# Attention and a routed expert layer on one core: two-sided buckets, spare matmuls, V loads behind q, new planner costs, and two expert tiles moved into the attention

## The chip, the cores and the metric

The kernel runs on one core of a Trainium2 chip. TensorE (PE) multiplies, VectorE (DVE) and ScalarE (ACT) work on vectors, GpSimd (POOL) and SyncE (SP) here mostly issue DMAs; POOL has its own DMA queue (the software one), SP another. The metric is device time in microseconds of one execution, lower is better.

## The reference

q, k, v are (8 batches, 8 heads, 576 tokens, 64) in float32. The attention is causal by blocks of 64. Its output, one row of 512 values for each of 4608 tokens, goes through a layer of 8 experts of which each token takes two:

```
scores = (q @ k^T) / 8, where block(i) >= block(j), else -1e9
x = softmax(scores) @ v            # (4608, 512)
noisy = x @ w_gate + log1p(exp(x @ w_noise)) * noise      # (4608, 8)
two largest per token, their softmax = weights
out[t] = sum over both experts e: weight * (relu(x[t] @ w1[e]) @ w2[e])   # 512 -> 1024 -> 512
```

## The kernel before, in words

A class `Plan` (L19 to L153) is a list scheduler inside the kernel: every step is added with an engine, a cost in microseconds, a key (smaller goes first), what it comes after, and the places it takes or gives back in pools. `order` plays this through and emits all instructions in one fixed order for each engine. On the chip each engine follows its order and waits where something is late; the costs matter only through the order that they make.

**Attention.** Eight batches b0 to b7, two halves (b0 to b3, b4 to b7), pairs pb = b // 2. For a batch, POOL issues the loads of q and k (`load_qk` L328, L330, the last 64 tokens in `load_rest` L335) and SP those of V (`load_v` L342, L345); PE turns q and k (`turn` L385, `turn_rest` L404), ACT or DVE copy the turned tiles (L395, L397); PE makes scores (L435, L453), ACT their exponentials (L444, L459), DVE clears the masked blocks (L465), POOL or DVE cast V (L353), PE multiplies with V (`av_mm` L480, L490), DVE divides (L500). The buffers `raw` for q and k number four, so two batches of them. V of b0 is loaded at once.

**Routing.** Of each batch x is turned (L512), copied (L521), and multiplied with the gate (L530). With each second batch the pair's 1152 tokens are routed on DVE (top2 L554 to L562, rows L583 to L592, shares L607 to L613) with `places` on PE (L569), which counts the tokens ahead of each one in its expert. Then POOL issues 18 scatters of 128 rows (`scatter` L627), 72 in all, into one bucket per expert and half in device memory (`xd`, 640 rows = five tiles, filled from row 0). The rows from 512 on are cleared first (`clear_x` L640).

**Experts.** 16 steps (half, e), in the order (0,0), (0,1), (0,2), (0,3), (1,0) to (1,3), (0,4), (1,4) and so on. A step loads its bucket (`load_x`, SP, L652), after all scatters of its half; PE turns it (`row_turn` L660), ACT or DVE copy (L670, L672); layer 1 is eight groups of 4 x 2 matmuls of 320 columns (L718), each with a relu (L727); layer 2 is, for each of five tiles, eight matmuls of 512 columns (L734). For every tile the result is scaled and stored (`y_early` L742 on ACT, two of them on DVE, `y_store` L749) if the expert is not the last, and, if it is not the first, the result that the token's other expert stored is gathered (`gather` L756, POOL), added (`y_late` L767, DVE) and written to the output rows (`y_out` L774, POOL). Rows for which a tile is the wrong side are dropped by an index out of bounds. So 70 tiles are stored, 70 gathered, 70 written out. A flag (L789 on) sends the program into a second, slow branch (L816) if a bucket overflowed.

What sets the order around the change: the keys of `load_qk`, `load_v` and `scatter`, the rule that a step is emitted when its inputs are ready by the planned costs, and in-order queues. In the places where PE works for experts before the attention is over there is nothing: no expert step starts before its half is scattered.

## Time and profile before

| what | value |
|---|---|
| three timed runs | 466.64, 472.96, 477.19 us (median 472.96) |
| profiled execution | 466.68 us, span 465.0 us, mean granted PE clock 0.971 |
| PE busy | 421.0 us, 91% of the span |
| ACT, POOL, DVE busy | 274.8, 272.7, 196.0 us |
| DMA moved | 96.24 MB, mean 207 GB/s |

The page gives each engine's busy time over one span, the span in 40 slices, the DMA queues, the chain that ended last, and the costliest groups of instructions by line. The windows cut the span at times that can be chosen. The attention ends at about 157 us; the expert steps without it run from there to the last matmul at 458 us.

### The profile page before, as it was taken

The page shows a single profiled execution, that of the slowest core. Times are in us where ns is not written, and L with a number is a line of the kernel's source. Part 1 is how long each engine was busy: PE and PEld are TensorE (multiplying, and loading weights), DVE is VectorE, ACT ScalarE, POOL GpSimd, SP SyncE. Part 2 cuts the span into 40 slices and gives each one's busy share as a digit, 9 for nine tenths or more (in the row PEclk, how much of TensorE's full clock was granted, in tenths as well). Part 3 has the DMA queues.
Part 4 walks back from the last instruction along what each step waited for, and adds up shares of the span by engine and source line. Part 5 has one row for each costly group of instructions (what it writes and reads, how often), then busy time and mean ns, then how long its engine had stood idle before and what let it go on. Part 6 is the DMA issues. An engine that isn't in the chain of part 4 may idle for free.

```text
span 465.0 us, 11045 instructions
## 1 busy us (share of the span) xinstructions
PE 421.0 (91%) x4409; PEld 271.9 (58%) x4431; DVE 196.0 (42%) x516; ACT 274.8 (59%) x364; POOL 272.7 (59%) x311
## 2 busy tenths in 40 slices
...
GB/s 164 185 168 189 241 239 223 204 200 222 192 249 236 226 271 247 296 146 229 208 200 203 211 152 188 181 218 219 291 225 271 303 169 207 229 147 228 135 65 102
DMA packets 108858, 96.24 MB, mean 207 GB/s; under 512 B 62944, under 2 KB 83424, under 8 KB 108800
## 3 DMA queue, kind: packets, MB, share of 16 engines
...
q14 instruction: 22, 0.18, 0.1%
...
## 4 chain that ended last, share of the span: by engine, by line
PE 65%; DMA 12%; DVE 10%; ACT 5%; issue 4%; POOL 2%; SPq 2%; POOLq 0%; DVEq 0%; ACTq 0%
PE yp L734 27%; PE hp L718 26%; DMA row<-xd 7%; ACT esc L444 4%; PE tr L660 3%; PE av L480 3%; DVE xr L500 2%; DMA raw<-in_q_dram 2%; PE sc L435 2%; DMA nz_all<-in_moe_noise_dram 2%; DVE Tq L397 2%; DMA vst<-in_v_dram 1%; POOL out_dram L774 1%; PE tr L385 1%; PE av L490 1%
## 5 line engine op out<-in xcount | busy, mean ns | idle before, releaser
L718 PE MATMUL hp<-xg,w 128*128 128x320 bf16 x1024 | 147.4, 299 | 0.1
L734 PE MATMUL yp<-w,hsb 128*128 128x512 bf16 x618 | 140.3, 379 | 1.2
L727 ACT ACTIVATE hsb<-hp 128x640 bf16<-128x640 f32 x127 | 89.4, 704 | 59.3 <-PE hp L718 58.1
L718 PEld LDWEIGHTS <-w 128*128 128x128 bf16 x1024 | 98.8, 98 | 39.9 <-issue 0.3
L734 PEld LDWEIGHTS <-hsb 128*128 128x128 bf16 x640 | 62.2, 97 | 73.3 <-issue 3.5
L444 ACT ACTIVATE esc<-sc 128x1024 bf16<-128x1024 f32 x96 | 92.3, 1027 | 15.1 <-PE sc L435 6.0
L627 POOL DMA_INDIRECT xd<-xr,slots x72 | 71.4, 992 | 35.0 <-issue 18.6
L774 POOL DMA_INDIRECT out_dram<-yobuf,trow x42 | 41.2, 980 | 29.1 <-DVE yobuf L767 20.7
L742 ACT ACTIVATE ybuf<-yp,wrow 128x512 f32<-128x512 f32 x42 | 28.9, 687 | 43.2 <-PE yp L734 43.2
L672 DVE COPY xg<-tr 128x1024 bf16<-128x1024 bf16 (+1 forms) x28 | 16.2, 577 | 87.9 <-PE tr L660 87.9
L774 POOL DMA_INDIRECT out_dram<-xr,trow x28 | 28.3, 1011 | 41.4 <-DVE xr L767 29.0
L756 POOL DMA_INDIRECT gbuf<-yd,grow x34 | 35.0, 1029 | 25.6 <-DMA yd<-xr 13.8
L435 PE MATMUL sc<-Tq,Tk 64*128 64x512 bf16 (+4 forms) x320 | 39.7, 326 | 9.9 <-ACT esc L444 7.2
L756 POOL DMA_INDIRECT xr<-yd,grow x36 | 37.1, 1030 | 11.8 <-issue 10.6
L480 PE MATMUL av<-vt,esc 128*128 128x65 bf16 x640 | 33.0, 208 | 9.0 <-DVE xr L500 4.7
L480 PEld LDWEIGHTS <-esc 128*128 128x128 bf16 x640 | 26.5, 106 | 20.4 <-DVE xr L500 6.5
L500 DVE TENSOR_TENSOR xr<-av,rden 128x256 bf16<-128x256 f32 (+1 forms) x80 | 33.9, 424 | 3.9 <-DMA xd<-xr,slots 1.0
L742 ACT ACTIVATE xr<-yp,wrow 128x512 f32<-128x512 f32 x26 | 17.9, 688 | 27.8 <-PE yp L734 25.7
L385 PE MATMUL tr<-ident,raw 128*64 128x128 bf16 x512 | 22.5, 239 | 10.5 <-POOL tok_i L304 7.3
L767 DVE SCALAR_TENSOR_TENSOR yobuf<-yp,wrow,xr 128x512 f32<-128x512 f32 x22 | 16.5, 751 | 26.4 <-ACT xr L742 17.6
L385 PEld LDWEIGHTS <-raw 128*64 128x64 bf16 x512 | 17.7, 120 | 14.8 <-DMA raw<-in_q_dram 8.3
L767 DVE SCALAR_TENSOR_TENSOR yobuf<-yp,wrow,gbuf 128x512 f32<-128x512 f32 x20 | 15.0, 750 | 25.0 <-ACT xr L742 13.8
...
## 6 DMA issues: line engine op xcount, KB each, us to landing
...
```

Source lines behind the costliest of these rows:

```text
L385: nc.tensor.transpose(tp[64 * f:64 * f + 64, r * P:(r + 1) * P], raws[b, x][:, o:o + D], ident)
L435: nc.tensor.matmul(out=sc[:, f, off:off + z - a], lhsT=kT[sl, m * S + jt * P:m * S + (jt + 1) * P], rhs=qT[sl, m * S + a:m * S + z], start ...
L444: nc.scalar.activation(out=escs[b, st][:, mm, :, piece * 512:(piece + 1) * 512], in_=scs.pop((b, m, piece)), func=AF.Exp, scale=scale)
L480: nc.tensor.matmul(out=av[:, f, mm, :], lhsT=esc[:, mm, f, c:c + P], rhs=vb[:, jt, h, :], start=(jt == 0), stop=(jt == idx))
L500: nc.vector.tensor_tensor(out=xrs[b // 2][sl, t, 0:Dm].rearrange("p (f m d) -> p f m d", f=2, m=HP)[:, :, 2 * st:2 * st + 2], in0=av[sl, : ...
L627: ins = nc.gpsimd.indirect_dma_start(out=xd[half].bitcast(I32), out_offset=bass.IndirectOffsetOnAxis(ap=slots[:, pb * TG + t, i:i + 1], ax ...
L718: nc.tensor.matmul(out=hp[:, n, 0:NW], lhsT=wload[e, 1][:, db, fb * P:(fb + 1) * P], rhs=xgs[half, e][:, db, n * NW:(n + 1) * NW], start=( ...
L727: nc.scalar.activation(out=o, in_=i, func=AF.Relu)
L734: nc.tensor.matmul(out=yp, lhsT=hs[half, e][:, fb, c * P:(c + 1) * P], rhs=wload[e, 2][:, fb, :], start=(fb == 0), stop=(fb == FB - 1))
L742: nc.scalar.activation(out=t, in_=yps[half, e, c], func=AF.Copy, scale=w)
L756: ins = nc.gpsimd.indirect_dma_start(out=g, out_offset=None, in_=yd[half][0:e * CAP], in_offset=bass.IndirectOffsetOnAxis(ap=grow[half][:, ...
L774: ins = nc.gpsimd.indirect_dma_start(out=out, out_offset=bass.IndirectOffsetOnAxis(ap=trow[half][:, e, c:c + 1], axis=0), in_=yos.pop((hal ...
```

## The change

Each token now has a lower and a higher expert (`roles`). In the lower one's bucket it fills rows from the bottom, in the higher one's from the top (places with a sign, `sg`). So a tile of a bucket holds rows of one kind, and limits by expert (`TE`, `TL`) say which tiles are stored and which gathered: 23 of each half, 46 in all, where there were 70. The stored rows lie closer (`YB`). The gap in the middle of a bucket is cleared (160 rows, `GAP`), in b0 and b4. A bucket beyond these limits sends the program into the slow branch.

The planner gets a hop by engine, starting times, and lower PE costs. Where PE would stand idle by the plan, and before the first turn, it puts in a `spare` matmul of ones, 128x512, into the PSUM tile that the next step takes (52 in all, 14 of them ahead of the first turn; the last is in the middle of b5). V of b0 waits for q's second chunk (the other wait, `RV`, is set so that it never applies). Pair 0's scatters get a later key and pair 1's an earlier one, against the other work on POOL. `FIRST = ((0, 2),)`: after pair 0's scatters SP loads the first two tiles of expert 0, half 0 (`load_first`); they are turned, and go through layer 1 (32 matmuls of 256 columns) and layer 2, in b5 to b7; the step (0,0) then does three tiles.

```diff
-    HOP = 0.08
+    HOP = {None: 0.0, "PE": 0.2, "ACT": 0.16, "DVE": 0.13, "POOL": 0.12, "SP": 0.08}
...
+    BEGIN = {"SP": 0.8, "DVE": 1.0, "POOL": 1.3, "ACT": 2.1}
...
-    ZR = 512
+    CR = 160
+    TL = (0, 1, 2, 3, 3, 4, 5, 5)
+    TE = TL[::-1]
+    YB = [P * sum(TE[:e]) for e in range(E + 1)]
...
+    FIRST = tuple((e, n) for e, n in ((0, 2), (1, 0)) if n)
...
+            if (b, idx) == (0, 0):
+                tc.add_manual_dep(ins.ins, loads[0, "q", 1].name, SYNC_DEP, reason="the first q and k go first")
...
+    begun = {}
+
+    def av_tile(name):
+        return begun.pop("av", None) or av_ps.tile([P, 512], F32, tag="av", name=name)
+
+    def sc_tile(name):
+        return begun.pop("sc", None) or sc_ps.tile([P, 2, 512], F32, tag="sc", name=name)
+
+    def spare(x):
+        if x not in begun:
+            begun[x] = av_tile("sp") if x == "av" else sc_tile("sp")
+        o = begun[x] if x == "av" else begun[x][:, 0]
+        nc.tensor.matmul(out=o, lhsT=ones_mat, rhs=ones_mat.unsqueeze(1).to_broadcast([P, 4, P]), start=True, stop=True)
...
+    def roles(pb):
+        r = rs["p", pb]
+        cd = rt.tile([P, 2, TG, E], BF16, tag="cd", name="cd")
+        nc.vector.tensor_tensor(out=cd, in0=r["oh"], in1=code.to_broadcast([P, 2, TG, E]), op=ALU.mult)
+        cc = rt.tile([P, 2, TG], F32, tag="cc", name="cc")
+        nc.vector.reduce_sum(cc, cd, axis=AX.X)
+        sel = rt.tile([P, TG, 2, 1], F32, tag="sel", name="sel")
+        nc.vector.tensor_tensor(out=sel[:, :, 0, 0], in0=cc[:, 0], in1=cc[:, 1], op=ALU.min)
+        nc.vector.tensor_tensor(out=sel[:, :, 1, 0], in0=cc[:, 0], in1=cc[:, 1], op=ALU.max)
+        sg = rt.tile([P, TG, 2, E], BF16, tag="sg", name="sg")
+        nc.vector.tensor_tensor(out=sg, in0=sel.to_broadcast([P, TG, 2, E]), in1=code.to_broadcast([P, TG, 2, E]),
+                                op=ALU.is_equal)
+        nc.vector.tensor_scalar(sg[:, :, 1], sg[:, :, 1], -1.0, None, op0=ALU.mult)
+        r.update(sg=sg, cc=cc)
...
-        pp = av_ps.tile([P, TG, E], F32, tag="av", name="pp")
-        nc.tensor.matmul(out=pp, lhsT=prem, rhs=m, start=True, stop=False)
+        sg = r["sg"].rearrange("p t i e -> p t (i e)")
+        pp = av_tile("pp")[:, 0:2 * TG * E].rearrange("p (t e) -> p t e", t=TG)
+        nc.tensor.matmul(out=pp, lhsT=prem, rhs=sg, start=True, stop=False)
         for t in range(TG - 1):
             nc.tensor.matmul(out=pp[:, t + 1:TG, :], lhsT=ones_mat,
-                             rhs=m[:, t:t + 1, :].to_broadcast([P, TG - 1 - t, E]), start=False, stop=False)
...
+        pk = rt.tile([P, TG, 2, E], F32, tag="pk", name="pk")
+        nc.vector.tensor_tensor(out=pk, in0=r["sg"], in1=r["pp"].rearrange("p t (i e) -> p t i e", i=2), op=ALU.mult)
         sl2 = rt.tile([P, TG, 2], F32, tag="sl2", name="sl2")
-        nc.vector.reduce_sum(sl2.rearrange("p t i -> p i t"), pk, axis=AX.X)
-        rec = xrs[pb][:, :, Dm:DR].bitcast(I32)
-        nc.vector.tensor_copy(slots[:, g0:g0 + TG, :], sl2)
-        nc.vector.tensor_copy(rec[:, :, 0:2], sl2)
+        nc.vector.reduce_sum(sl2, pk, axis=AX.X)
+        nc.vector.scalar_tensor_tensor(out=slots[:, g0:g0 + TG, :], in0=sl2, scalar=-1.0, in1=sl2,
+                                       op0=ALU.mult, op1=ALU.max)
+        nc.vector.tensor_copy(xrs[pb][:, :, Dm:DR].bitcast(I32)[:, :, 0:2], slots[:, g0:g0 + TG, :])
...
+    GAP = [min(max(4 * (S // 4 * (E - 1 - e) // (E - 1)) - 48, 0), CAP - CR) for e in range(E)]
 
     def clear_x(half, e):
-        flat = xd[half].rearrange("(e r) c -> e r c", e=E)[:, ZR:CAP, :].rearrange("e (p a) c -> e p (a c)", a=4)
-        nc.sync.dma_start(out=flat[e], in_=zeros[e % 4])
+        r0 = e * CAP + GAP[e]
+        nc.sync.dma_start(out=xd[half][r0:r0 + CR, :].rearrange("(p a) c -> p (a c)", a=4), in_=zeros[e % 2])
...
+    def load_first():
+        t = row_pool.tile([P, CT * Dm], BF16, tag="row", name="row")[:, 0:len(early) * DR].rearrange("p (c d) -> p c d", d=DR)
+        rowss["first"], mine = t, []
+        for e, n in FIRST:
+            k = early.index((e, 0))
+            ins = nc.sync.dma_start(out=t.bitcast(I32)[:, k:k + n, :], in_=xd[0].bitcast(I32)[e * CAP:e * CAP + n * P, :]
+                                    .rearrange("(c p) d -> p c d", p=P))
+            mine.append(ins.ins)
+            for nm in scat_of[0]:
+                tc.add_manual_dep(ins.ins, nm, SYNC_DEP, reason="rows landed")
+        for i in mine:
+            tc.add_to_no_dep_group("scat0", i)
...
+    def load_x(half, e, c0):
         t = row_pool.tile([P, CT, Dm], BF16, tag="row", name="row")
-        landed(nc.sync.dma_start(out=t, in_=xd[half][e * CAP:(e + 1) * CAP, 0:Dm]
+        landed(nc.sync.dma_start(out=t[:, c0:CT, :], in_=xd[half][e * CAP + c0 * P:(e + 1) * CAP, 0:Dm]
...
+    def layer1(half, e, fb, c0, c1):
+        if fb == 0 and c0 == 0:
             hs[half, e] = h_pool.tile([P, FB, CAP], BF16, tag="hsb", name="hsb")
-        hp = sc_ps.tile([P, 2, 512], F32, tag="sc", name="hp")
+        hp = sc_tile("hp")
         for db in range(DB):
-            for n in range(2):
...
+                nc.tensor.matmul(out=hp[:, i, 0:n], lhsT=wload[e, 1][:, db, fb * P:(fb + 1) * P],
+                                 rhs=xgs[half, e][:, db, a:a + n],
                                  start=(db == 0), stop=(db == DB - 1))
...
     def y_store(half, e, c):
-        r0 = e * CAP + c * P
+        r0 = YB[e] + c * P
...
     def gather(half, e, c):
         g = spot("g")
         ins = nc.gpsimd.indirect_dma_start(
-            out=g, out_offset=None, in_=yd[half][0:e * CAP],
+            out=g, out_offset=None, in_=yd[half][0:YB[e]],
             in_offset=bass.IndirectOffsetOnAxis(ap=grow[half][:, e, c:c + 1], axis=0),
-            bounds_check=e * CAP - 1, oob_is_err=False)
+            bounds_check=YB[e] - 1, oob_is_err=False)
...
-                pe = add("PE", 0.58, lambda b=b, x=x, c=c: turn(b, x, c), after=[turned[x, c], o_new, o_ident],
+                key = u0 + 3 * c * (b == 0) - 5
+                pe = add("PE", 0.46, lambda b=b, x=x, c=c: turn(b, x, c), after=[turned[x, c], o_new, o_ident],
...
-                s = rest[b] = add("PE", 0.4, lambda b=b: scores_rest(b), key=key, take=["sc"], after=list(got.values()))
+                s = rest[b] = add("PE", 0.25, lambda b=b: scores_rest(b), key=key, take=["sc"], after=list(got.values()))
...
-                pe = add("PE", (0.22, 0.33, 0.45, 0.56, 0.68)[idx], lambda b=b, st=st, idx=idx: av_mm(b, st, idx),
-                         after=need_v + [mk], key=key + 3 + 0.1 * idx, take=["av"])
+                pe = add("PE", (0.12, 0.24, 0.35, 0.47, 0.6)[idx], lambda b=b, st=st, idx=idx: av_mm(b, st, idx),
+                         after=need_v + [mk], key=key + 2 + 0.1 * idx, take=["av"])
...
-            if b == (1, 2)[hf]:
-                cleared[hf] = [add("SP", 0.3, lambda hf=hf, e=e: clear_x(hf, e), key=u0 - 10 + e,
-                                   after=[units[b, (2, 0)], o_vec], xfer=(0.41, 165)) for e in range(E)]
+            if b == (0, 4)[hf]:
...
+            t2 = add("DVE", 1.3, lambda pb=pb: top2(pb), after=[noi[b - 1], noi[b], o_cast], key=kr - 20)
+            ro = add("DVE", 0.9, lambda pb=pb: roles(pb), after=[t2], key=kr - 20)
...
-            ss = [add("POOL", 1.28, lambda pb=pb, t=t, i=i: scatter(pb, t, i), after=[routed, *cleared[half]], key=kr + (0, 20, 10, 0)[pb],
+            ss = [add("POOL", 1.28, lambda pb=pb, t=t, i=i: scatter(pb, t, i), after=[routed, *cleared[half]], key=kr + (20, -30, 0, 0)[pb],
                       xfer=(0.36, 165))
...
-    weights(0, lambda: wE, [units[2, (m, 0)] for m in range(4)], unit(6, 0), calm=1)
-    weights(1, lambda: wE, [units[5, (m, 0)] for m in range(4)], unit(6, 0) + 1, calm=2)
+        ra = add("DVE", 0.9, lambda half=half: read_rec_a(half), key=unit(6, 0), after=[lr, done_b[half], o_cast])
+        rec_ops[half] = add("DVE", 1.2, lambda half=half: read_rec_b(half), key=unit(6, 0), after=[ra])
+    weights(0, lambda: wE, [units[3, (m, 0)] for m in range(4)], unit(6, 0), calm=4)
+    weights(1, lambda: wE, [units[6, (m, 0)] for m in range(4)], unit(6, 0) + 1, calm=4)
...
-    weights(3, lambda: wl["R"], [scat_ops[1][18 + n] for n in (0, 3, 6, 9)], unit(6, 0) + 3, [o_right], calm=4)
+    weights(3, lambda: wl["R"], [scat_ops[1][18 + n] for n in (4, 7, 10, 13)], unit(6, 0) + 3, [o_right], calm=4)
...
-        kb = 1000 + 20 * sn
-        lx = add("SP", 1.0, lambda half=half, e=e: load_x(half, e), key=unit(6, 6) + sn, take=["row"],
-                 after=scat_ops[half], behind=[last_x], xfer=(2.0, 45), late=1.0)
+        kb = 1000 + 20 * sn - (0 if sn == 0 else 900 if sn == 1 else 0)
+        cut = dict(FIRST).get(e, 0) if half == 0 else 0
+        if sn == 0 and cut:
+            first_x = add("SP", 1.0, load_first, key=unit(2, 6), after=scat_ops[0][0:2 * TG], take=["row"], xfer=(1.2, 60), late=1.0)
...
+            used = [first_w]
+        lx = add("SP", 1.0, lambda half=half, e=e, cut=cut: load_x(half, e, cut), key=unit(5, 6) + sn, take=["row"],
+                 after=scat_ops[half], behind=[last_x], xfer=(0.4 * (CT - cut), 45), late=1.0)
...
-        o_x = add(None, 0, key=kb, take=["xg"], after=[lx, last_xg])
+        o_x = add(None, 0, key=kb, take=["xg"], after=[first_x if cut else lx, last_xg])
...
-            pl.ops[r]["fn"] = lambda half=half, e=e, j=j, r=r: row_copy(half, e, j, pl.ops[r]["by"])
-            xcs.append(r)
...
+        for c0, c1 in ((0, cut), (cut, CT)) if cut else ((0, CT),):
...
+                n = min(2, c1 - j)
+                cs = list(range(j, j + n))
+                pe = add("PE", 0.225 * n, lambda half=half, e=e, cs=cs: row_turn(half, e, cs), key=kb - 15 + 0.05 * j,
+                         after=[first_x if c1 <= cut else lx, o_x], take=["tr"])
...
+            w = (c1 - c0) / CT
+            rl[c0] = []
+            for fb in range(FB):
+                pe = add("PE", 0.02 + 1.07 * w, lambda half=half, e=e, fb=fb, c0=c0, c1=c1: layer1(half, e, fb, c0, c1),
+                         key=kb + fb + 0.1 * c0, after=[*xcs, *wop[e][1], o_h], take=["sc"])
+                l1.append(pe)
...
-        if e:
-            for c in range(CT):
+        if TL[e]:
+            for c in range(CT - TL[e], CT):
                 gs[c] = add("POOL", 1.32, lambda half=half, e=e, c=c: gather(half, e, c), key=kb + c, take=["g"],
                             after=st_ops[half] + [rec_ops[half]], behind=[last_g], xfer=(0.5, 85), late=2.2)
...
         for c in range(CT):
             pe = add("PE", 1.75, lambda half=half, e=e, c=c: layer2(half, e, c), key=kb + 10 + c,
-                     after=rl + wop[e][2], behind=[last_2], take=["av"])
+                     after=rl[cut if c >= cut else 0] + wop[e][2], behind=[last_2] if c >= cut else [], take=["av"])
...
             fin = []
-            if e < E - 1:
-                ye = add(("ACT", "DVE") if sn < 4 else "ACT", (0.6, 0.75) if sn < 4 else 0.6, None, after=[pe, rec_ops[half]], key=500 + kb + c, take=["y"])
+            if c < TE[e]:
+                ye = add(("ACT", "DVE") if sn < 4 else "ACT", (0.6, 0.75) if sn < 4 else 0.6, None, after=[pe, first_w if c < cut else rec_ops[half]], key=500 + kb + c, take=["y"])
...
-            if e:
+            if c >= CT - TL[e]:
                 yl = add("DVE", 0.75, lambda half=half, e=e, c=c: y_late(half, e, c),
                          after=[pe, gs[c], rec_ops[half]], key=500 + kb + c, take=["yo"], give=["g"])
```

**PE, start of the program.** `raw` is q and k as loaded, `sp` the spare tile. Before:

```order
L1275 UNCONDITIONAL_BRANCH
L385 LDWEIGHTS raw
L385 MATMUL tr<-ident,raw 64x128
```

Now:

```order
L1406 UNCONDITIONAL_BRANCH
L419 LDWEIGHTS ones_mat
L419 MATMUL sp<-ones_mat 128x512
...
L426 LDWEIGHTS raw
L426 MATMUL tr<-ident,raw 64x128
```

Fourteen spare matmuls stand ahead of the first turn.

**POOL, the loads of q and k for b5 to b7 and the scatters.** `xd` is the bucket, `raw` and `rest` are q and k, `w` expert weights. Before, from pair 0's scatters on (the first loads are those of b5):

```order
L627 DMA xd<-xr,slots 5120x260 x18
L328 DMA raw<-in_q_dram 128x2x1024
L328 DMA raw<-in_k_dram 128x2x1024
L335 DMA rest<-in_q_dram 32x2x512
L335 DMA rest<-in_k_dram 32x2x512
...
L627 DMA xd<-xr,slots 5120x260 x3
...
L627 DMA xd<-xr,slots 5120x260 x9
L328 DMA raw<-in_q_dram 128x2x1024
L328 DMA raw<-in_k_dram 128x2x1024
L627 DMA xd<-xr,slots 5120x260 x6
```

Now:

```order
L681 DMA xd<-xr,slots 5120x260 x9
L350 DMA raw<-in_q_dram 128x2x1024
L350 DMA raw<-in_k_dram 128x2x1024
L681 DMA xd<-xr,slots 5120x260 x9
L360 DMA rest<-in_q_dram 32x2x512
...
L681 DMA xd<-xr,slots 5120x260 x18
L350 DMA raw<-in_q_dram 128x2x1024
L350 DMA raw<-in_k_dram 128x2x1024
```

The loads of b5 stand behind nine of pair 0's scatters instead of 18; those of b7 behind all 18 of pair 1's instead of twelve. Between the two pieces shown last stand the loads of b6 and four of weights.

**PE, the first tiles of expert 0 inside the attention** (now; before there is nothing of the kind). `sc` are scores, `esc` their exponentials, `xg` turned rows, `hp` the hidden layer:

```order
L476 MATMUL sc<-Tq,Tk 128x192
L737 LDWEIGHTS row
L737 MATMUL tr<-ident,row 128x128
...
L521 LDWEIGHTS esc
L521 MATMUL sp<-vt_140,esc 128x65
...
L800 LDWEIGHTS w_1556
L800 MATMUL hp<-xg,w_1556 128x256
```

Eight turns stand together in b5, 32 matmuls of layer 1 spread over the end of b6, 16 of layer 2 in two groups in b7.

## Rows read from the trace of the kernel before

**Rows 1.** Section 1 of the page: busy time, share of the span, instructions.

```profile
PE 421.0 (91%) x4409; PEld 271.9 (58%) x4431; DVE 196.0 (42%) x516; ACT 274.8 (59%) x364; POOL 272.7 (59%) x311
```

**Rows 2.** Windows: us, PE, PEld, DVE, ACT, POOL busy, PEclk, DMA, GB/s.

```profile
0.00:157.50 157.50, 122.48 (x2357) 88.85 (x2358) 112.72 (x345) 119.58 (x146) 88.78 (x124) 0.92 1.05 209
176.00:458.00 282.00, 280.73 (x1848) 170.55 (x1868) 73.56 (x132) 146.10 (x205) 168.84 (x172) 1.00 0.76 206
458.00:465.00 7.00, 0.31 (x2) 0.00 (x0) 0.75 (x1) 0.00 (x0) 1.59 (x2) 0.75 0.18 61
```

**Rows 3.** Lines by form, whole span: count | busy us, mean ns | idle before.

```profile
L587 DVE TENSOR_TENSOR pk<-oh,pos 128x144 f32<-128x144 bf16 x4 | 1.2, 307 | 0.1
L459 ACT ACTIVATE esc<-sc 128x256 bf16<-128x256 f32 x8 | 3.1, 385 | 0.0
L727 ACT ACTIVATE hsb<-hp 128x640 bf16<-128x640 f32 x127 | 89.4, 704 | 59.3 <-PE hp L718 58.1 <-PE fs L805 0.4
L742 ACT ACTIVATE ybuf<-yp,wrow 128x512 f32<-128x512 f32 x42 | 28.9, 687 | 43.2 <-PE yp L734 43.2
L756 POOL DMA_INDIRECT gbuf<-yd,grow x34 | 35.0, 1029 | 25.6 <-DMA yd<-xr 13.8 <-issue 11.7
```

**Rows 4.** The chain of waits: start, us, engine, tile, line, in the dense stage.

```profile
205.23 8.41 PE yp L734 x38
213.65 6.52 PE hp L718 x48
...
220.16 0.89 PE tr L660 x16
```

**Rows 5.** Timeline at the end, POOL: start, us, engine, operation.

```profile
459.38 0.97 POOL L774 DMA_INDIRECT out_dram<-yobuf,trow  x1 [0.76 <-DVE yobuf L767]
```

**Rows 6.** Timeline at the start, SP, POOL, PE, ACT.

```profile
0.82 3.15 SPq L342 DMA_DIRECT2D vst<-in_v_dram  x4
1.36 0.90 POOL L330 DMA_DIRECT2D raw<-in_q_dram  x1 [0.83 <-POOLq L1264]
7.26 1.06 PE L385 MATMUL tr<-ident,raw 128*64 128x128 bf16 x16 [7.26 <-POOL tok_i L304]
13.67 1.07 PE L385 MATMUL tr<-ident,raw 128*64 128x128 bf16 x16
13.74 1.94 ACT L444 ACTIVATE esc<-sc 128x1024 bf16<-128x1024 f32 x2
16.67 0.62 POOL L353 CAST vt<-vst 128x512 bf16<-128x512 f32 x1
21.07 0.84 PE L480 MATMUL av<-vt,esc 128*128 128x65 bf16 x12
```

**Rows 7.** Timeline, loads of q and k, scatters, ACT's waits, a turn.

```profile
90.53 0.78 POOL L328 DMA_DIRECT2D raw<-in_q_dram  x1
96.50 1.08 POOL L627 DMA_INDIRECT xd<-xr,slots  x1 [0.76 <-DVE ms L612]
100.62 1.02 ACT L395 ACTIVATE Tq<-tr 128x1024 bf16<-128x1024 bf16 x1 [2.46 <-PE tr L385]
106.27 4.69 ACT L444 ACTIVATE esc<-sc 128x1024 bf16<-128x1024 f32 x5 [1.35 <-PE sc L435]
107.40 1.07 POOL L627 DMA_INDIRECT xd<-xr,slots  x1 [0.30 <-issue]
118.86 0.78 POOL L328 DMA_DIRECT2D raw<-in_q_dram  x1
130.93 0.64 PE L385 MATMUL tr<-ident,raw 128*64 128x128 bf16 x16
```

**Rows 8.** Windows in which the granted clock was low, columns as in group 2.

```profile
92.50:103.50 11.00, 9.35 (x138) 7.03 (x135) 7.69 (x31) 7.26 (x9) 6.32 (x9) 0.53 1.14 199
123.50:127.50 4.00, 3.83 (x62) 3.08 (x59) 2.98 (x10) 2.35 (x3) 3.09 (x4) 0.57 1.15 207
137.00:144.50 7.50, 6.89 (x108) 4.90 (x109) 6.11 (x27) 4.70 (x6) 3.10 (x4) 0.54 1.15 226
```

326 lines of the change are left out of this document (190 added, 136 removed).

## The prediction, made blind

> **What bounds the kernel now.** I read the busy times first, then the windows by stage, then the chain of waits, then the timeline of the places that the change touches. PE is busy 421.0 us and no other engine over 275 [rows 1], but that is a mean over two different stages. In the stretch 176 to 458 us PE works 280.73 of 282 us at the full granted clock, while ACT has 146.1 and POOL 168.8 [rows 2]: the expert steps are bound by PE alone, and the chain runs through their matmuls there [rows 4]. In the attention, 0 to 157.5 us, nobody is full: PE 122.5, ACT 119.6, DVE 112.7, POOL 88.8, DMA share 1.05 and 209 GB/s, mean clock 0.92 [rows 2]. The reader should see from this that a piece of work taken from ACT, POOL or SP after 176 us is worth nothing, a matmul taken from there is worth its time, and what changes in the attention is worth what its own chain says.
>
> **The sum** is made against the profiled execution (466.68 us, span 465.0). The median of the three timed runs, 472.96, lies 6.3 above it; as the runs reach from 466.6 to 477.2 I add half of that, 3.1, to a profiled time.
>
> *Fewer stores, gathers and writes of y.* 24 tiles less of each: 24 evictions of 0.69 us on ACT, 24 gathers of 1.03 and about as long a write each on POOL [rows 3, 5], some 49 us of POOL. All of it lies under the 280.73 us of PE; POOL has 113 us free there [rows 2]. **0.** At the end the last matmul is over before the stretch 458 to 465, and what follows (an addition, writes from POOL, the last 0.97 long at 459.38, their landing) remains [rows 2, 5]: 0 as well. If the cover were gone, two writes in the tail would cost 2 us.
>
> *The first two tiles.* The dense stage loses 8 turns (16 take 0.89, so 0.45), two fifths of layer 1 of one step (eight groups of 8 matmuls: 48 matmuls take 6.52 us, so 64 take 8.7 and two fifths 3.48) [rows 4], and two of five tiles of layer 2, 16 matmuls of which 38 take 8.41, 3.5 [rows 4]. Together 7.4 us, all on the path. In the attention they need PE 7.4 us, of which PE has 35 free by 157.5 [rows 2], and on ACT up to 8 relus (0.39 for a 256-wide exponential to 0.70 for the 640-wide relu, the nearer to the first), two scalings of 0.69 and a copy of about 1.0 [rows 3, 7]: 0 to 5.5 us if ACT were the bound. The eight relus may also go to DVE. I take 2. **−5.4** (0 to −7.4). The load of these rows stands on SP, behind it four of b6's V loads; it waits for pair 0's last scatter, which before was over by 90.5 [rows 7], with two whole batches of attention still ahead: 0.
>
> *Start.* Before, V of b0 leaves at 0.82, half a microsecond before q and k [rows 6]; the first turn starts at 7.26 and ACT's first exponential at 13.74. With V behind q's second chunk the first q and k have the DMA engines to themselves; V has until 16.67, when the first cast begins, or 21.07, the first V matmul [rows 6]. The fourteen spare matmuls run before anything else can. In this stretch 16 turns take 1.07 us, at 130.93 the same 16 take 0.64 [rows 6, 7], so the start runs as at the lower level whatever the row of granted clock says, and 64 turns at full speed are worth 1.7 us. The start can gain 0 (bounded by the q load alone) to 5.5 us (both). **−4.0**: the first exponential near 10.
>
> *q and k of b5.* Their loads stand behind nine scatters instead of 18: 9 x 1.33 (a scatter and its gap, from rows like 107.40) = 12 us earlier. Before they left at 90.53 and ACT stood still for 2.46 us for their turns and 1.35 for the first scores [rows 7]: 0 to −3.8. **−3.0**, because the rest follows nine more scatters as before.
>
> *Stretches of low clock.* In three stretches, 22.5 us together, the granted clock is 0.53 to 0.57, the lower of the two levels, while PE is busy 20.1 us [rows 8]. At the higher level that work takes half, but ACT, DVE and DMA (share 1.14 and 1.15) stand beside it. Thirty-eight spares, put in where the plan has PE idle, keep it occupied; a full gain would be 10 us, none is possible. They take the place of idle time, and as the step behind takes the same PSUM tile, a spare that starts late delays by at most its own length, 0.22 us by group 4's 38 matmuls, twice that at the lower level. I take **−4.0** (0 to −10), less than half, because the stretches are as much DMA as PE.
>
> *Routing.* Per pair DVE gets ten small operations more (seven in `roles`, three in the shares) and loses three; the nearest row is 0.307 us for one of 144 wide [rows 3], the largest of them, so seven more come to 1 to 2 us, and four pairs to 4 at the lower figure. DVE is at 72% [rows 2] and only what stands ahead of a pair's scatters can be on a path. **+1.0** (0 to 4). Smaller clears of the buckets come earlier, and no row of before waits for one: 0.
>
> Sum: −5.4 − 4.0 − 3.0 − 4.0 + 1.0 = −15.4, so 451.3 for a profiled execution and with 3.1 more **454 us**. With the ends of the terms it would be 443 to 474; terms do not all fall on one side, so the case's own range is 447 to 461.
>
> As a check, q and k of b7, which stand now behind all 18 scatters of pair 1: before, its scatters began at 96.50, stopped until 107.40 and the load left at 118.86, its turn stood at 130.93, 12.1 later [rows 7]. If pair 1 begins about 4 us earlier (the start's gain), at 92, 18 x 1.33 = 24 later is 116: a turn at 128, earlier than before.
>
> **A rule that speaks against a term.** The stretch at 137.0 is low right behind the turns at 130.93 [rows 7, 8], so turns may be what lets the clock fall, and spares between them may not be enough; the stretch at 123.5 ends before them and is low too, so they are not the whole cause. If they were, the clock term would be 0 and the start's 1.7 would go: that is rival C. By the Trainium skill, "TensorE: Matmul & The Clock Gate", Part 4: PE-mode transpose, a transpose does not count as PE-busy in the way that a matmul does. By that rule the time would be C's; the stretch at 123.5 agrees with it only in part.
>
> **The rivals.**
>
> A, the forecast: 447 to 461, **46%**.
>
> B, better: the attention packs down to ACT. ACT has 119.6 us of work in it [rows 2], plus up to 5.5 for the tiles. If all of b1 to b7 ran at ACT's rate, the attention would take its 125 us and the first 10 without an exponential, 135, which is 22 less; less 5.4 for the tiles and plus 3.1, from 466.7, that is 442: 437 to 447, about 443. For it: PE, ACT and DVE are all under 80% busy there, so all of their holes are the order's. Against: DMA share 1.05. **15%**.
>
> C, the clock is not kept and the order, built on costs of the higher level, waits where PE is slow: the clock term 0, the start −2, b5 −1 and the tiles −5.4, with +1: −7.4, so 459 and with 3.1 of the median 462; range 458 to 465. For it: the stretch at 137.0; against: 52 spares of 0.44 are 23 us more of PE's work, in which it isn't idle. **18%**, two thirds of it under 463.5.
>
> D, the attention is bound by DMA: 209 GB/s over 157.5 us are 32.9 MB that nothing in the change removes (V, q, k, weights and scatters are all still there), and the DMA share stands at 1.05 over the whole of it [rows 2]. Then the start, b5 and the clock give nothing and the tiles alone remain: 466.7 − 5.4 + 3.1 = 464.4, about 465, and 462 to 469 with their bounds. **10%**. At the start the loads of V and q leave within half a microsecond of each other [rows 6]. The Trainium skill, "DMA: Bandwidth & Descriptors", Queues, rings and completion order, says that each engine takes turns between the queues that it has work for; the late first turn at 7.26 agrees, and no row here shows the turns themselves.
>
> E, slower: q and k of b7 come too late. They stand behind six scatters more than before, 8 us of POOL. If the first of pair 1 leaves not at 92 but at 107.4, where before they went on [rows 7], the load leaves at 131.3 and the turn stands at 143.4 instead of 130.93. That is 12.5 us of a stop; less the 5.4 of the tiles, plus 3.1, 477. Each microsecond more of delay adds one: from about 113 on it is 2% slower. For it: pair 1's places wait on more DVE work. Against: pair 1's key is earlier now. **10%**, of it 6 past 2% slower.
>
> F, the slow branch is taken because a bucket passes its limits or the first pair fills less than two tiles of expert 0: far slower, beyond any figure here. Worked out from the reference's own routing, the counts lie inside (288 rows for the two tiles of 256, 598 of 640 in expert 0). **1%**.
>
> **Numbers.** 2% of 473 is about what a measurement here can tell from no change: faster is below 463.5, slower above 482.4. Faster: A 46, B 15 and 12 of C, 73%. Same: 6 of C, D's 10, 4 of E: 20%. Slower: 6 of E and F: 7%. The range 441 to 469 leaves out the low tail of B and most of E.
>
> **What would show it.** Fifty-two spares on PE; the first exponential at about 10 and not 13.7; the first turn of tiles and layer 1 of 256 columns inside the attention; the load of b7 before 118.9; the start of the dense stage more than 8 us before 176, with PE busy in it by 7.4 us less; the clock in the slices of the attention up; POOL's busy time down by about 49, with no effect; after the last matmul still 6.7 us. It would be wrong if the attention's end moves by less than 8 us, and most wrong if the turns of b7 come after 131.

## The result, and the profile after

The changed kernel takes **472.68 us** (median of 20 runs, 468.42 to 476.98) against 467.21 for the kernel before on the same chip (20 runs, 464.93 to 479.95). The ratio is 1.0092 with an interval of 1.0065 to 1.0120: about 4.3 us slower, which a limit of 2% calls the same. The forecast was 454 us, faster, and its range ended at 469. Runs came in two conditions, and in one of them both kernels take 75 to 85 us more (543 to 555 against 467 to 472 us for the kernel before), so a ratio is only set beside a ratio of the same condition, called here the usual and the long one.

The profiled execution took 476.02 us with a span of 474.1, some 3 above the median; that of before had 465.0 of span [rows 1 to 8 are from it]. The 9.1 us between the spans are what has to be found; as this execution is one of the longer ones, they are about twice what the ratio says (4.3). First the busy times on the page of the changed kernel, to be held against [rows 1]:

```profile
PE 431.3 (91%) x4484; PEld 272.7 (58%) x4484; DVE 182.3 (38%) x569; ACT 261.9 (55%) x351; POOL 224.2 (47%) x262
```

POOL has 48.5 us less to do, as forecast, and ACT 12.9 and DVE 13.7 less; PE has 10.3 more, the spares. Three engines lighter and the kernel slower: the reader should take from it that no sum of work explains the result. The windows of the changed kernel (us, PE, PEld, DVE, ACT, POOL busy, granted clock, DMA share, GB/s), beside [rows 2]:

```profile
0.00:157.50 157.50, 132.31 (x2381) 90.32 (x2381) 109.89 (x352) 118.27 (x151) 82.31 (x116) 0.93 1.03 206
157.50:176.00 18.50, 17.66 (x258) 13.76 (x259) 13.74 (x53) 14.40 (x20) 13.62 (x15) 1.00 0.77 207
176.00:464.00 288.00, 280.60 (x1845) 168.56 (x1844) 57.94 (x165) 129.26 (x181) 126.31 (x130) 0.99 0.71 186
```

In the attention (the first window) PE is 9.8 us busier and the mean granted clock is 0.93 where it was 0.92. To see where the time goes, one mark per batch is enough: the last small group of scores of each batch, which PE runs in order. These are the marks of b5, b6 and b7 in the timeline of the kernel before, and then of the changed one (start, us, engine, operation):

```profile
111.04 0.31 PE L453 MATMUL sc<-Tq,Tk 64*64 64x64 bf16 x8
128.23 0.31 PE L453 MATMUL sc<-Tq,Tk 64*64 64x64 bf16 x8
147.81 0.31 PE L453 MATMUL sc<-Tq,Tk 64*64 64x64 bf16 x8
```

```profile
114.93 0.31 PE L494 MATMUL sc<-Tq,Tk 64*64 64x64 bf16 x8
130.03 0.31 PE L494 MATMUL sc<-Tq,Tk 64*64 64x64 bf16 x8
154.12 0.31 PE L494 MATMUL sc<-Tq,Tk 64*64 64x64 bf16 x8
```

All eight marks, before and after: 19.19 and 15.06, 38.05 and 39.41, 55.88 and 54.77, 71.16 and 74.45, 90.58 and 88.62, 111.04 and 114.93, 128.23 and 130.03, 147.81 and 154.12. The changed kernel is ahead by 4.1 us at b0, behind at b1, ahead at b2, behind at b3, ahead at b4, and then behind for good. It gains three times and gives it back each time. From b7's mark to the end of the last matmul it is 310.5 us before and 310.6 after, and from there to the end of the span 6.7 and 9.4. So 6.3 + 0.1 + 2.7 = 9.1.

**The start** (timeline of the changed kernel, beside [rows 6]; in brackets the idle time ahead of an instruction and what ended it):

```profile
1.14 4.91 PE L419 MATMUL sp<-ones_mat 128*128 128x512 bf16 x14 [1.14 <-DVE ones_mat L311]
5.98 0.64 PE L426 MATMUL tr<-ident,raw 128*64 128x128 bf16 x16
8.59 8.04 SPq L367 DMA_DIRECT2D vst<-in_v_dram  x4
10.22 5.60 ACT L485 ACTIVATE esc<-sc 128x1024 bf16<-128x1024 f32 x6
20.17 0.43 DVE L381 CAST vt<-vst 128x512 bf16<-128x512 f32 x1 [3.69 <-DMA vst<-in_v_dram]
20.65 0.54 PE L521 MATMUL av<-vt,esc 128*128 128x65 bf16 x7 [3.85 <-DVE vt L381]
21.78 1.02 ACT L485 ACTIVATE esc<-sc 128x1024 bf16<-128x1024 f32 x1 [3.54 <-PE sc L476]
```

The first exponential stands at 10.22 and not 13.74, 3.52 us earlier, and 16 turns take 0.64 us and not 1.06. (The row of granted clock reads 1.00 over the first 14 us in both kernels, so only these lengths tell the two starts apart.) But V's four loads, now issued from 8.59 on over 8.04 us and not from 0.82 over 3.15, are late: the first cast of V still comes in time, at 12.75, but the second, at 20.17, PE and ACT each wait 3.5 to 3.9 us. The gain is gone some twelve microseconds after it was made. The run without the tiles, below, has the same wait (4.56, 4.16 and 4.67 us), so it isn't a feature of this one execution.

**From b3 to b7** (POOL, DVE, PE and ACT in the changed kernel, in order of time):

```profile
69.70 0.62 POOL L381 CAST vt<-vst 128x512 bf16<-128x512 f32 x1 [5.98 <-DMA vst<-in_v_dram]
71.99 1.10 POOL L681 DMA_INDIRECT xd<-xr,slots  x1 [0.30 <-DVE rden L540]
83.33 0.83 POOL L350 DMA_DIRECT2D raw<-in_q_dram  x1
90.30 1.08 PE L426 MATMUL tr<-ident,raw 128*64 128x128 bf16 x32
95.88 0.97 POOL L681 DMA_INDIRECT xd<-xr,slots  x1 [0.30 <-DMA xd<-xr,slots]
101.00 0.42 DVE L541 TENSOR_TENSOR xr<-av,rden 128x256 bf16<-128x256 f32 x1 [1.61 <-DMA rest<-in_q_dram]
101.47 0.28 PE L623 MATMUL pp<-sg,prem 128*128 128x144 bf16 x1 [2.92 <-DVE xr L541]
106.17 1.07 POOL L681 DMA_INDIRECT xd<-xr,slots  x1 [0.30 <-DVE base L674]
107.38 1.94 ACT L485 ACTIVATE esc<-sc 128x1024 bf16<-128x1024 f32 x2 [9.27 <-PE av L531]
131.57 0.79 POOL L350 DMA_DIRECT2D raw<-in_q_dram  x1
142.67 1.08 PE L426 MATMUL tr<-ident,raw 128*64 128x128 bf16 x32
```

The same two ends of pair 0's scatters in the timeline of the kernel before:

```profile
63.63 1.11 POOL L627 DMA_INDIRECT xd<-xr,slots  x1 [0.44 <-DVE ms L612]
89.55 0.97 POOL L627 DMA_INDIRECT xd<-xr,slots  x1 [0.30 <-issue]
```

Read it downwards. A cast of V on POOL waits 5.98 us for its load, and in POOL's queue two loads of weights and pair 0's scatters, which have a later key now, stand behind it: the first scatter leaves at 71.99 and not 63.63, the last at 95.88 and not 89.55. The load of b5, now after nine of them, leaves at 83.33 and not 90.53, and its first turns stand at 90.30. Before, PE's first group of them was at 99.51. That is 9 us gained. But b4's first output on DVE comes only at 101.00; PE's matmuls for pair 1's places wait 2.92 us on it, with the V matmuls behind them, and ACT, whose exponentials need the tiles that those V matmuls free, stands still for 9.27 us before 107.38. The whole gain of b5 is lost in that one stop, and the run without the tiles has it too (9.62 us before 107.49). Pair 1's scatters begin at 106.17 (before 96.50 [rows 7]), and b7's load, behind all 18 of them, leaves at 131.57 (before 118.86); its turns stand at 142.67 (before 130.93).

Why is DVE late at 101.00? The row names the transfer of q's last rows, which landed in the same tenth of a microsecond, but this output reads nothing of q. By the code it writes the one of two row buffers from which pair 0's scatters read, and DVE's wait ends at 100.76, right behind the last of these scatters, which was issued at 95.88 and landed at 100.68. In the kernel before, that scatter was issued at 89.55 and landed at 95.06, b4's first output came at 96.83, and the view of its line names the scatter for the only wait (us, times):

```profile
  DMA xd<-xr,slots: 1.0, 1
```

So it is pair 0's late scatters that hold b4's output, by the row buffer, and through it pair 1's places. No run here had a third buffer to test it by.

The stop has a second part. PE is nearly without work before 101.40, and then works at the lower level of its clock (columns as in the windows above):

```profile
98.50:101.40 2.90, 0.06 (x4) 0.08 (x1) 1.12 (x6) 0.00 (x0) 2.30 (x4) 0.80 0.99 219
101.40:107.70 6.30, 5.42 (x98) 4.89 (x99) 4.71 (x24) 0.32 (x1) 3.09 (x5) 0.50 1.07 169
```

At the higher level the 5.42 us of matmuls would be about half as long, so some 2.7 of ACT's 9.27 us are the clock, an estimate from these rows.

**The dense stage** (timeline of the changed kernel, POOL and PE):

```profile
212.10 1.07 POOL L843 DMA_INDIRECT xr<-yd,grow  x1 [0.30 <-issue]
218.12 3.57 PE L817 MATMUL yp<-w,hsb 128*128 128x512 bf16 x8 [6.06 <-DVE xr L854]
```

In the kernel before the first gather left at 198.37. Here it stands behind the last scatters in POOL's queue and leaves at 212.10, PE waits 6.06 us for the addition that needs it, and then eight matmuls take 3.57 us where they elsewhere take 1.89. Without those 7.7 us the stretch from b7's mark to the last matmul would be 302.9, shorter than before by 7.6, which is near the tiles' work that was moved out of it (7.4). But not all of it is the tiles: without the tiles, in the run below, this stretch is 307.4, already 3.1 shorter than before, and with them but without the spares 303.6, so the tiles have about 4 of it. Where the rest comes from isn't shown. The other runs in the usual condition have 0 to 2 us of waiting in this place, so most of the 6.06 us belong to this one execution, which was 3.3 us over the median.

**The end.** After the last matmul there are 9.4 us and not 6.7. The views of waits from 440 us on (who waits <- for whom: us, times, longest) give for the changed kernel, and then for the one before:

```profile
SPq L1406 <- PEq L1406: 4.4, 2, 3.9
```

```profile
SPq L1275 <- PEq L1275: 1.7, 2, 1.2
```

The four variants of the change in the usual condition, below, have 9.3 to 9.7. The 2.7 us are at the close of the program, when SP waits for PE's queue; what makes them I did not find.

### The profile page after: what moved, and what is told of

It reads as the page before. It is cut to its first block, busy times and chain, and to the rows that moved or that the text cites. A ratio compares the mean times of both kernels' runs of the same rounds, so it can differ in the third digit from the quotient of the medians.

```text
span 474.1 us, 10961 instructions
## 1 busy us (share of the span) xinstructions
PE 431.3 (91%) x4484; PEld 272.7 (58%) x4484; DVE 182.3 (38%) x569; ACT 261.9 (55%) x351; POOL 224.2 (47%) x262
## 4 chain that ended last, share of the span: by engine, by line
PE 33%; issue 25%; POOL 20%; DMA 12%; DVE 4%; ACT 3%; POOLq 1%; SPq 0%; DVEq 0%; ACTq 0%
PE yp L817 14%; PE hp L800 13%; POOL xd L681 9%; POOL out_dram L861 4%; DMA xd<-xr,slots 3%; POOL xr L843 3%; ACT esc L485 2%; DMA vst<-in_v_dram 2%; POOL gbuf L843 2%; POOL w L402 2%; PE tr L737 2%; DMA rest<-in_k_dram 2%; PE sc L476 1%; PE av L521 1%; DMA raw<-in_q_dram 1%
## 5 line engine op out<-in xcount | busy, mean ns | idle before, releaser
L800 PE MATMUL hp<-xg,w 128*128 128x320 bf16 (+2 forms) x1024 | 149.7, 300 | 1.7 <-ACT esc L485 0.8
L810 ACT ACTIVATE hsb<-hp 128x640 bf16<-128x640 f32 (+2 forms) x133 | 89.8, 677 | 98.6 <-PE hp L800 97.7
L485 ACT ACTIVATE esc<-sc 128x1024 bf16<-128x1024 f32 x95 | 91.5, 1028 | 20.8 <-PE sc L476 10.3
L861 POOL DMA_INDIRECT out_dram<-yobuf,trow x27 | 27.0, 1002 | 56.6 <-DVE yobuf L854 52.6
L476 PE MATMUL sc<-Tq,Tk 64*128 64x448 bf16 (+3 forms) x318 | 36.2, 303 | 8.7 <-ACT esc L485 7.9
L829 ACT ACTIVATE ybuf<-yp,wrow 128x512 f32<-128x512 f32 x27 | 18.6, 687 | 28.6 <-PE yp L817 24.7
L843 POOL DMA_INDIRECT gbuf<-yd,grow x22 | 22.8, 1038 | 20.5 <-DMA yd<-xr 13.7
L843 POOL DMA_INDIRECT xr<-yd,grow x24 | 24.8, 1034 | 7.3 <-issue 7.3
L402 POOL DMA_DIRECT2D w<-in_moe_w_dram x32 | 24.9, 789 | 1.4 <-DMA w<-in_moe_w_dram 1.4
L476 PEld LDWEIGHTS <-Tk 64*128 64x128 bf16 x320 | 12.8, 95 | 21.0 <-issue 14.7
L737 PE MATMUL tr<-ident,row 128*128 128x128 bf16 x320 | 23.3, 219 | 0.5 <-ACT xg L747 0.2
```

What stands on the lines that cost most here:

```text
L402: nc.gpsimd.dma_start(out=t[:, part * n:(part + 1) * n], in_=src.rearrange("(b p) f -> p b f", p=P)[:, part * n:(part + 1) * n])
L476: nc.tensor.matmul(out=sc[:, f, off:off + z - a], lhsT=kT[sl, m * S + jt * P:m * S + (jt + 1) * P], rhs=qT[sl, m * S + a:m * S + z], start ...
L485: nc.scalar.activation(out=escs[b, st][:, mm, :, piece * 512:(piece + 1) * 512], in_=scs.pop((b, m, piece)), func=AF.Exp, scale=scale)
L737: nc.tensor.transpose(tp[:, db, i, :], r[:, db * P:(db + 1) * P], ident)
L800: nc.tensor.matmul(out=hp[:, i, 0:n], lhsT=wload[e, 1][:, db, fb * P:(fb + 1) * P], rhs=xgs[half, e][:, db, a:a + n], start=(db == 0), sto ...
L810: nc.scalar.activation(out=o, in_=i, func=AF.Relu)
```

## The experiments

The theory was: the gains are real, and the order in POOL's queue hands them back (V's cast ahead of the scatters, nine more scatters ahead of b7's load). The rivals: a part of the change costs by itself (the tiles in the attention, the spares, DVE's work on roles); or the new order as a whole is worse, in no single place.

**In the usual condition** (kernel before 467 to 472 us) four variants of the changed kernel ran. Positions of their profiled executions, in us:

| kernel | ratio to before | pair 0's first, last scatter | pair 1's first | b7's load | b7's mark |
|---|---|---|---|---|---|
| before | 1 | 63.63, 89.55 | 96.50 | 118.86 | 147.81 |
| changed | 1.0092 [1.0065, 1.0120] | 71.99, 95.88 | 106.17 | 131.57 | 154.12 |
| no tiles | 1.0187 [1.0129, 1.0244] | 71.18, 95.18 | 106.26 | 129.14 | 155.82 |
| no spares | 1.0193 [1.0122, 1.0264] | 71.08, 94.76 | 112.16 | 135.13 | 162.29 |
| old keys and casts | 1.0289 [1.0218, 1.0360] | 67.00, 88.85 | 115.86 | 131.61 | 161.42 |
| old plan | 1.0189 [1.0076, 1.0302] | 66.81, 88.90 | 104.60 | 124.94 | 156.87 |

*No tiles in the attention:*

```diff
-    FIRST = tuple((e, n) for e, n in ((0, 2), (1, 0)) if n)
+    FIRST = tuple((e, n) for e, n in ((0, 0), (1, 0)) if n)
```

> No tiles of expert 0 during the attention (FIRST empty); everything else as changed. Theory (the tiles are only moved: b7 is as much later as the dense stage is shorter, since PE has no idle time at b6 and b7 that others could not use): the rest scores of b7 come 4 to 6 us earlier, the dense stage is 7 us longer, time within 2 us of the changed kernel's. Rival (the tiles are worth their 5.4 us and the loss lies elsewhere): 4 to 6 us slower than the changed kernel.

It measured 475.37 us against 467.19. Its ratio less that of the change is 0.0095: to leave the tiles out costs 4.4 us, give or take 3 (forecast for the tiles 5.4). The mark of b7 doesn't come earlier without them (155.82), so they cost the attention nothing that shows. The forecast of this run was missed, and the rival that the tiles are the loss falls. The plan also gives another order from the middle of the attention on when they are left out, so the 4.4 hold the tiles and the new order together.

*No spare matmuls:*

```diff
-    pl.spare = dict(fn=spare, cost=(0.22, 0.43), after=1.3, **{"in": ("av", "sc")}, share=0.6, cold=turn_first, till=last_score[-1])
+    pl.unused = dict(fn=spare, cost=(0.22, 0.43), after=1.3, **{"in": ("av", "sc")}, share=0.6, cold=turn_first, till=last_score[-1])
```

> No spare matmuls; everything else as changed, the planner's order included as far as it does not hang on them. Theory (the spares only fill idle time, and the clock is lost at the stops anyway): time within 2 us of the changed kernel, first turns at the lower clock again. Rival 1 (they keep the clock): 3 to 6 us slower. Rival 2 (they hold up the steps behind them): 2 to 5 us faster.

It measured 476.38 us against 467.19, so to leave the spares out costs 0.0101, 4.7 us, give or take 3.5; the forecast was missed here too. This figure isn't the spares alone: without them the plan gives all engines another order from b1 on (POOL, for one, has one load of weights ahead of pair 0's scatters and not two), and an order by itself was worth 4 us in the last experiment below. Its first turns on PE, in the timeline:

```profile
5.53 1.06 PE L426 MATMUL tr<-ident,raw 128*64 128x128 bf16 x16 [5.53 <-DMA raw<-in_q_dram]
```

They take 1.06 us each time in the first 11 us, with the spares 0.64 each time; yet the first exponential comes at 10.35, against 10.22. So the early exponential is the work of V's later load, not of the spares. What these and the order made with them give comes after: the marks of b1, b3 and b4 stand at 42.18, 79.89 and 96.98, against 39.41, 74.45 and 88.62 with them. The granted clock in 0 to 157.5 us is 0.92 here and 0.93 there; the mean hides what the marks show.

*The old keys of the scatters, and V of b3 and b4 cast by DVE*, to take away both of POOL's suspected waits:

```diff
-            n = cast[idx] = add(("POOL", "DVE"), (0.55, 0.42) if idx < 4 else (0.6, 0.5), None,
+            n = cast[idx] = add(("POOL", "DVE") if b not in (3, 4) else ("DVE",), ((0.55, 0.42) if idx < 4 else (0.6, 0.5))[0 if b not in (3, 4) else 1:], None,
...
-            ss = [add("POOL", 1.28, lambda pb=pb, t=t, i=i: scatter(pb, t, i), after=[routed, *cleared[half]], key=kr + (20, -30, 0, 0)[pb],
+            ss = [add("POOL", 1.28, lambda pb=pb, t=t, i=i: scatter(pb, t, i), after=[routed, *cleared[half]], key=kr + (0, 20, 10, 0)[pb],
```

> The kernel with old keys and DVE's casts once more, for a chip on which PE does not wait for instructions (there the kernel before takes 467). Theory (POOL's order makes both stops): ACT's stop of 9 us before b5 gone, b7's rest scores at 142 to 148, time 455 to 462. Rival: 468 or more.

It measured 484.38 us against 471.96: slower than the change by 0.0197, 9.3 us, where a faster kernel was expected. The theory falls here in the form that I gave it. Pair 0's scatters do end at 88.85, as before; but pair 1's begin at 115.86. The window 100 to 120 us (columns as above) and two rows of its timeline, PE and POOL, show what is in the way now:

```profile
100.00:120.00 20.00, 12.29 (x171) 7.17 (x172) 11.45 (x46) 4.05 (x6) 4.92 (x7) 0.68 0.96 213
```

```profile
107.17 0.62 PE L521 MATMUL av<-vt,esc 128*128 128x65 bf16 x8 [5.01 <-DVE noisy L589]
109.89 0.61 POOL L381 CAST vt<-vst 128x512 bf16<-128x512 f32 x1 [16.51 <-DVE sg L614]
```

ACT is busy 4.05 of 20 us. PE's V matmuls wait 5.01 us behind DVE's routing with the noise, whose load stands on SP behind V's. Between the marks of b3 and b4 lie 37 us. After that each batch takes only 14 to 16.5 us (115.15, then 131.62, 145.70, 161.42). The stop has moved to another engine's queue and grown.

*The planner's costs, keys and dependences as before*, on top of the new buckets, roles, tiles and spares:

```diff
-    HOP = {None: 0.0, "PE": 0.2, "ACT": 0.16, "DVE": 0.13, "POOL": 0.12, "SP": 0.08}
+    HOP = {None: 0.0, "PE": 0.08, "ACT": 0.08, "DVE": 0.08, "POOL": 0.08, "SP": 0.08}
...
-    BEGIN = {"SP": 0.8, "DVE": 1.0, "POOL": 1.3, "ACT": 2.1}
+    BEGIN = {}
...
-                key = u0 + 3 * c * (b == 0) - 5
-                pe = add("PE", 0.46, lambda b=b, x=x, c=c: turn(b, x, c), after=[turned[x, c], o_new, o_ident],
+                key = u0 + 3 * c * (b == 0) - 1
+                pe = add("PE", 0.58, lambda b=b, x=x, c=c: turn(b, x, c), after=[turned[x, c], o_new, o_ident],
...
-            ss = [add("POOL", 1.28, lambda pb=pb, t=t, i=i: scatter(pb, t, i), after=[routed, *cleared[half]], key=kr + (20, -30, 0, 0)[pb],
+            ss = [add("POOL", 1.28, lambda pb=pb, t=t, i=i: scatter(pb, t, i), after=[routed, *cleared[half]], key=kr + (0, 20, 10, 0)[pb],
```

> The planner's costs, hops and starting times, the keys and marks (scatters, V, casts, clears, weights) and V of b0 at once, all as before the change; kept are the two-sided buckets with their 46 stores, gathers and writes, the roles on DVE, the tiles of expert 0 in the attention, and the spares that this plan leaves (21). Order on POOL then nearly as before. Theory (the new order of loads and scatters is what gives the gain back; the tiles are worth 4 us): b7's rest scores at 146 to 150, 2 to 8 us faster than the kernel before, so 8 to 13 faster than the changed one. Rival 1 (the order is no worse, the roles and buckets cost it): as slow as the changed kernel. Rival 2 (the attention ends when its 31 MB are moved, whatever the order): within 2 us of the kernel before less the tiles' 4.

It measured 479.47 us against 472.14. Its interval overlaps with that of the change, so the two aren't told apart, and the gain that was expected did not come; it is slower than the kernel before, with nearly the order of before. Two rows of its timeline, SP's queue and PE, show new parts that the old order has no room for:

```profile
59.99 13.70 SPq L695 DMA_DIRECT2D xd<-gbuf  x8
100.07 0.28 PE L621 MATMUL sp<-sg,prem 128*128 128x144 bf16 x1 [2.58 <-DVE sg L614]
```

The larger clears (160 rows of a bucket and not 128) hold SP's queue for 13.70 us (7.62 in the kernel before) and the load of b4's V behind them until 73.79; and PE waits 2.58 us for the longer work on roles. So in this order the new buckets have a price in the attention, which the forecast put at 1 us for the roles and 0 for the clears. In the changed kernel the clears stand elsewhere, in b0 and spread over 96 to 140 us, and their price there isn't shown.

**In the long condition** (kernel before 543 to 555 us) the other runs stand. They compare with the first of them, the change as it is:

> The changed kernel itself, for an undisturbed profile beside the next three. Theory (handed back on queues): the three stops of its first trace are there again: ACT waits 9 us about 98 to 107 us because the first outputs of b4 go into the row buffer that pair 0's last scatters still read; PE waits 6 us about 212 to 218 us for the first gather of expert 1, which stands behind pair 3's scatters on POOL; V of b0 comes after 20 us and holds PE 4 us. Time 472. Rival (the clock and the spare matmuls): the stops are those of a disturbed execution, smaller here, and PE's busy time in the attention is higher than before by 10 us or more instead.

546.31 against 544.83, ratio 1.0052 [1.0018, 1.0085]: about the same verdict as in the usual condition. The time of 472 us did not come. Of the three stops that were expected, the wait for V (3.48 us on ACT) and ACT's stop ahead of b5 (8.08 us before 124.25) are there; PE's for the first gather is only 1.38 us.

*V of b0 loaded at once*, as before, in two runs:

```diff
-            if (b, idx) == (0, 0):
-                tc.add_manual_dep(ins.ins, loads[0, "q", 1].name, SYNC_DEP, reason="the first q and k go first")
```

> V of b0 no longer waits for q; order unchanged. Theory: the first exponential is late again, near 13 us, but V's casts don't wait 4 us, so b1's rest scores stand within 1 us of the changed kernel's 39.4; time within 1 us of it. Rival (V behind q is a plain gain of 3.5 us): 3 to 4 us slower than the changed kernel.

> V of b0 does not wait for q, on this chip. Theory: the first exponential 2 to 4 us later than at 10.2, PE's wait of 4 us for V at 16.6 to 20.6 gone; b1's rest scores within 1.5 us of 39.4; time within 1.5 us of the changed kernel's. Rival (the start is worth its 3.5 us): 3 to 4 us slower.

0.9989 [0.9942, 1.0036] and 0.9937 [0.9890, 0.9984]: no worse than the change, perhaps 3 to 6 us better. In the first of them the first exponential comes at 13.31, as before, and still b1's mark is earlier. The rows are that mark here, and in the change as it is:

```profile
38.11 0.31 PE L492 MATMUL sc<-Tq,Tk 64*64 64x64 bf16 x8 [0.20 <-ACT esc L483]
```

```profile
40.12 0.31 PE L494 MATMUL sc<-Tq,Tk 64*64 64x64 bf16 x8 [0.20 <-ACT esc L485]
```

With V moved back the first exponential begins 3 us earlier and b1's mark comes 2 us later. In these two profiles, one of each kernel, the start's term is not only lost but turned round.

*V of b3 and b4 cast by DVE alone* (the first half of the edit above), in two runs:

> V of b3 and b4 is cast by DVE alone, so that on POOL pair 0's scatters don't stand behind casts that wait for V (six us at 63 to 70). Theory: pair 0's scatters start about 8 us earlier, the stop of 9 us at b4's outputs goes, b5's rest scores come at about 107 instead of 115; the time falls by 4 to 8 us against the changed kernel. Rival (PE and DMA bound the attention): the scatters start earlier and the attention ends where it did; within 1 us.

> V of b3 and b4 cast by DVE alone, as in the run on the other chip. Theory: pair 0's scatters start about 8 us sooner than at 72, ACT's stop of 9 us before b5 goes, pair 1's scatters start 5 us or more sooner than at 106; 4 to 8 us faster than the changed kernel. Rival (casts that wait on DVE hold DVE as they held POOL): b4 is later by what the scatters are sooner; within 1.5 us or slower.

1.0166 [1.0096, 1.0236] and 1.0127 [1.0079, 1.0174], slower than the change. In the first, pair 0's last scatter goes at 89.79 and not 92.64, but pair 1's first at 127.60 and not 122.23. Both forecasts were missed: POOL's wait taken away didn't bring pair 1 forward.

*The second half of pair 1's 18 scatters after b7's load* (pair 1's keys from −30 to 20, so that the load stands behind nine), in two runs:

```diff
-            ss = [add("POOL", 1.28, lambda pb=pb, t=t, i=i: scatter(pb, t, i), after=[routed, *cleared[half]], key=kr + (20, -30, 0, 0)[pb],
+            ss = [add("POOL", 1.28, lambda pb=pb, t=t, i=i: scatter(pb, t, i), after=[routed, *cleared[half]], key=kr + (20, 20, 0, 0)[pb],
```

> Pair 1's scatters get the key of pair 0's: on POOL the load of q and k of b7 now stands behind nine of them instead of 18; pair 0's part is unchanged. Theory (rival E of the prediction: b7 waits for its q and k behind pair 1's scatters, which start only at 106): the load leaves about 12 us sooner than at 131, b7's rest scores come 5 to 8 us sooner than at 154, and the time falls by 4 to 7 us against the changed kernel. Rival (b6 to b7 takes 24 us because PE and ACT are full of other work there): within 1.5 us.

> The same kernel as the run with b7's loads behind nine scatters, for the same reason. Where the kernel before takes 467: theory (rival E), b7's load leaves about 12 us sooner than at 131, its rest scores at 146 to 149 instead of 154, time 465 to 468. Rival (b7 is held by PE and ACT): 471 or more.

1.0156 [1.0066, 1.0246] and 1.0191 [1.0107, 1.0275]. In the second the mechanism works: these are pair 1's first scatter and b7's load in its timeline,

```profile
125.77 1.07 POOL L681 DMA_INDIRECT xd<-xr,slots  x1 [0.30 <-DVE base L674]
137.63 0.78 POOL L350 DMA_DIRECT2D raw<-in_q_dram  x1
```

11.9 us apart, where they are 25.4 apart in the change and 22.8 in the change as it is in this condition. Its load of b7 leaves 7.4 us earlier than in the change as it is (145.03), and b7's mark comes 27.5 us earlier (189.28 against 216.81); the total is slower all the same (559.0 us of span against 544.5). In 200 to 250 us PE is busy 29.83 us there and 42.51 in the change as it is, so the gain is lost behind b7. Both forecasts were missed, and an earlier load of b7 isn't worth its time by itself.

*The gathers of the second step, (0,1), ahead of what POOL has queued:*

```diff
-                gs[c] = add("POOL", 1.32, lambda half=half, e=e, c=c: gather(half, e, c), key=kb + c, take=["g"],
+                gs[c] = add("POOL", 1.32, lambda half=half, e=e, c=c: gather(half, e, c), key=kb + c - 200 * (sn == 1), take=["g"],
```

> The gathers of step (0,1) get a smaller key: one of them now stands ahead of the last ten scatters of pair 3 on POOL. Theory: PE's stop of 6 us in the second step goes, and with it the lower clock behind it: 5 to 8 us faster than the changed kernel. Rival (the sum of the stores, not POOL, is late, or the scatters that are later now hold half 1's steps): within 1 us.

1.0133 [1.0055, 1.0212]: no gain from it. The change as it is waits only 1.38 us at this place in the long condition, so the run says little of the 6.06 us of the profiled execution.

*The old keys of the scatters and the casts on DVE*, the same kernel as in the usual condition above, four times, and *the old keys alone*:

> The keys of the scatters as before the change, and V of b3 and b4 cast by DVE: pair 0's scatters together, q and k of b5 and b6 right behind them, q and k of b7 behind eight of pair 1's. Theory (both stops are the order of POOL's queue): both go, b7's rest scores stand at 142 to 148, and the time is 455 to 462, faster than both kernels. Rival (the rest of the change costs it): 468 or more.

> The same kernel as the run with the old scatter keys and DVE's casts; there the kernel before took 554 us and every engine waited for instructions while POOL scattered, so that its stops could not be read. Where the kernel before takes 467: theory (POOL's queue makes both stops), b5's rest scores at 105 to 109, b7's at 142 to 148, time 455 to 462. Rival (other parts of the change cost it): 468 or more.

> Third run of the kernel with the old scatter keys and DVE's casts, for a chip on which the kernel before takes 467. Theory (POOL's queue makes both stops of the attention): b5's rest scores at 105 to 109, b7's at 142 to 148, time 455 to 462. Rival (other parts of the change cost it): 468 or more.

> Old keys and V of b3 and b4 cast by DVE, on the same chip as the run with the keys alone. Theory: 3 to 6 us faster than that; where the kernel before takes 467, 455 to 462. Rival: no faster than the keys alone.

> The scatters' keys as before the change, V's casts as changed. Pair 0's 18 scatters stand together, b5's and b6's q and k behind them, b7's behind four of pair 1's. Theory (b7's loads behind pair 1's scatters are the larger part): b7's rest scores sooner by 5 to 8 us than the changed kernel's, the stop before b5 stays (the casts still hold POOL), 3 to 6 us faster than the changed kernel. Rival (the casts ahead of pair 0's scatters are the larger part): within 2 us of it.

0.9891 [0.9809, 0.9973], 0.9849 [0.9793, 0.9906], 0.9885 [0.9812, 0.9958] and 0.9928 [0.9853, 1.0003] with both; 1.0134 [1.0074, 1.0195] with the keys alone. The times of 455 to 462 us that were expected came in none of them. So this version is 0.7 to 1.5% faster than the kernel before in the long condition, and 2.9% slower in the usual one. No version here beats both kernels in the usual condition.

*The kernel before with the change's costs in its planner and nothing else* (an edit of the kernel before):

```diff
-    HOP = 0.08
+    HOP = {None: 0.0, "PE": 0.2, "ACT": 0.16, "DVE": 0.13, "POOL": 0.12, "SP": 0.08}
+    BEGIN = {"SP": 0.8, "DVE": 1.0, "POOL": 1.3, "ACT": 2.1}
...
-                pe = add("PE", 0.58, lambda b=b, x=x, c=c: turn(b, x, c), after=[turned[x, c], o_new, o_ident],
+                pe = add("PE", 0.46, lambda b=b, x=x, c=c: turn(b, x, c), after=[turned[x, c], o_new, o_ident],
```

> The kernel before, with nothing of the change but the planner's new PE costs, hops and starting times: same work, same keys, another order (on DVE 227 of 936 rows of the comparison differ). Theory (each order is a draw: where a load or a cast stands in an in-order queue costs several us, the order of before is one on which little stops, and any other loses 1 to 3% against it, which the change's gains only make up in part): 0.8 to 2.5% slower than before. Rival 1 (the new costs are nearer to the chip and make a better order): 0.5 to 1.5% faster. Rival 2 (the buckets' own work, roles and clears, is what costs it): within 0.5% of before.

548.53 us against 544.52, 1.0082 [1.0037, 1.0126]. The instructions are the same, only their order on the engines is another, and it costs about 4 us, in this condition. An order that is better by the planner's reckoning can be worse on the chip.

## Why the prediction was wrong

**The step that failed** is the sum over the attention: start −4.0, b5 −3.0 and clock −4.0 were added as if each gain stayed once it was made. With it failed the "check" that was to guard the sum: "If pair 1 begins about 4 us earlier (the start's gain), at 92". It began at 106.17: the start's gain was spent at V's wait, the gain of b5 at ACT's stop of 9.27 us. From there all goes as the check reckons, with its own rates: 25.4 us to b7's load (24 reckoned) and 11.1 to the turns (12.1).

Rival E is what happened, nearly to the number: pair 1 first at 107.4, load at 131.3, turn at 143.4; measured 106.17, 131.57 and 142.67. It had 10%. That it came so near is partly luck: 107.4 was the place where the scatters went on in the kernel before, taken over without a working, and the reason given for it, more DVE work, isn't what held pair 1. Its price was too high: it reckoned 12.5 us of a stop, and b7's mark came 6.3 later, since b7's steps pack more closely behind its turns (11.5 us from there to the mark, before 16.9). Against E the prediction held that pair 1's key is earlier now. A key sets the place in POOL's queue; what pair 1 waited for was the places' matmuls, and these waited for a DVE output of b4, late behind pair 0's scatters. The key could not move that.

Point by point:

- **First two tiles**, −5.4: about right: 4.4 us, give or take 3, by the run without them, and some 4 by the stretch behind b7's mark.
- **Start**, −4.0: the first exponential came as forecast (10.22 for "near 10") and the price of V was left out. [Rows 6] held it: V's first load left at 0.82 and it was cast from 16.67 on; the forecast gave it until then without asking when loads that begin 7.8 us later, and take 8.04 us and not 3.15 to issue, would have landed. The second cast had to wait until 20.17, and ACT's stop of 3.54 takes back the 3.52.
- **b5**, −3.0: the load was 7.2 us earlier and not 12, because pair 0's first scatter, behind V's cast and a later key, was 8.4 late, and nine scatters with their stops had taken 15.6 us before; its turns were even 9 us earlier; and the 9.27 us of ACT's stop took all of it.
- **Clock**, −4.0: 4.7 us, give or take 3.5, separate the change from the run without spares, but that run has another order too, so whether the size is right isn't shown. Against the kernel before nothing of it is left, and the mean granted clock moved from 0.92 to 0.93. Rival C, no clock and waits instead, happened in part: at the start the turns run in 0.64 us with fourteen spares ahead and in 1.06 without, but behind the stop at 101.40 the clock is at the lower level, 0.50, for 6.3 us and more. By the Trainium skill, "TensorE: Matmul & The Clock Gate", Part 4: PE-mode transpose, a transpose does not count as PE-busy in the way that a matmul does. The trace agrees in so far as turns alone stayed at 1.06 through the first 11 us, and shows besides that turns with a few spares between them keep 0.64.
- **Routing**, +1.0: DVE's work on roles went from 4.3 to 5.4 us a pair, so +1.1 a pair, for four pairs past the upper end of the range (4); what of it lay on a path isn't shown. The clears, put at 0, hold SP for 13.70 us in the old plan; in the changed kernel their price isn't shown.
- **Fewer stores and gathers**, 0: as far as the runs show right, with 48.5 us less of POOL and no gain; it was not tried alone. That POOL's first gather would be late wasn't seen: its free time of 113 us lay behind the scatters.
- **The tail**, "still 6.7": it was 9.4.
- **The median**, +3.1 over the profiled time: over 20 runs the kernel before has 467.21, only 0.5 above its profiled 466.68, so most of these 3.1 us were not there.
- **Rival D**, DMA: in the old keys and casts the DMA share fell to 0.89 in 0 to 157.5 us while the kernel got slower, so there it isn't more DMA that made it slower; for the change itself, with 1.03, no run took DMA work away, and it stays open.

**What stays open.** Of the parts that were taken out one by one in the usual condition, each made the kernel slower, or no different that can be told: tiles and spares, each with the order that comes with it, pay 4.4 and 4.7 us, and the old plan doesn't bring the kernel before's time back. What the tiles and the spares pay and the result together say that the rest of the change costs 13 us or so (4.3 + 4.4 + 4.7, if they add and if the orders that came with them are left aside). The chain from V's cast to ACT's stop is read from the rows; the runs that took waits out of it moved the stop and didn't win the time back, so how much of the loss it has isn't shown. The new order alone has a price of 4 us in the kernel before (in the long condition), V behind q perhaps 3 to 6 (in the long condition), the end 2.7. Buckets filled from both sides were not tried alone, and which part has the rest isn't shown.
